# A down projection by 26 products on blocks of 188 columns instead of 20 on 251, and where its sums and copies are issued

## Chip, cores and metric

The kernel runs on one core of a Trainium2 chip. The metric is the device time of one execution in microseconds, the median of several runs. The engines are TensorE (PE, with its weight loads shown apart as PEld), VectorE (DVE), ScalarE (ACT), GpSimd (POOL) and SyncE (SP), which issues the DMAs. TensorE reads its operands from SBUF and writes to PSUM banks; VectorE and ScalarE read and write both.

## What is computed

The reference, cut to what matters (all float32):

```python
# x: (8, 3008, 256), w_in: (256, 2048), w_out: (2048, 256)
X = np.fft.fft(x, axis=1)
X = np.fft.fft(X, axis=2)
x = X.real.reshape(8 * 3008, 256)
h = x @ w_in
g = np.maximum(0.01 * h, h)
return g @ w_out
```

So a two-dimensional Fourier transform of each of eight sequences, its real part, an up projection to 2048 features, a leaky ReLU and a down projection to 256.

## The kernel before, in words

**Up.** The transform along the features is folded into the weights once, at the start, so `wf` holds a cosine half and a sine half of the up projection. The real part of the transform at frequency k and at its mirror S - k are the sum and the difference of the same two products. Per unit (one of the 8 sequences and one parity of k, 16 units in all) the transform along the sequence leaves two tiles, `mixc` and `mixs`. The head of the kernel handles 502 columns of the first unit plainly (lines 864 to 917). All else is done in 31 *chunks* of up to 377 columns, two per unit except in the first. `Chunk.up` (line 1050) makes, for each of 16 blocks f of 128 hidden features, a cosine product and a sine product of 377 columns (line 1053); `seed` (line 1048) has put the Nyquist term into the cosine bank beforehand. ScalarE copies the cosine bank to SBUF (line 1061), and `hidden` (line 1064) has VectorE write copy + sine and copy - sine to the tile `block` (line 1075). One step later ScalarE applies the leaky ReLU in place (line 1324).

**Down.** A chunk gives 2 x 377 or 2 x 376 outputs. They are cut into 3 blocks of 251 columns; the 16 hidden blocks are taken as 4 groups of 4 (`divmod(f, 4)`: group k, row g), and the 256 outputs as 2 halves. The down projection is thus a product of a 2x4 by a 4x3 matrix of blocks, 24 block products, each of four rows g. It is done with 20, in the manner of Strassen: `W_SUMS` lists sums of weights (made once, line 651), `SUMS` the sums of hidden blocks, `PRODUCTS` triples of (weight, value, accumulator), and `COMBINED` the sums and differences of accumulators, of which `RESULTS` are the outputs.

- `sum` (line 1090) makes one sum of hidden blocks on GpSimd (line 1095), 4 x 251 = 1004 elements on 128 partitions. A sum is written over an operand that is used for the last time, or into a free slot. In the last chunk every third sum goes to VectorE.
- `product` (line 1101) makes one row of one product on TensorE (line 1112), 251 columns, into one half of one of three PSUM banks, `sum_psa`, `sum_psb`, `sum_psc`. The trace shows a float32 product as two records.
- `combine` (line 1121) is called when both accumulators of a bank are complete: ScalarE copies those in `COPIED` to SBUF (line 1128), and what can be combined goes on a list. `make` (line 1148) makes one combination on VectorE (line 1156), from PSUM or from SBUF. `leave` (line 1140) makes what is left in a bank before the bank is written again. `put` (line 1178) stores a result by DMA from SP.
- `Slots` (line 979) hands out 24 places in `block`: three adjacent ones for a group k, one for a sum.

**Transform along the sequence.** Beside this, x of the next sequence is loaded and folded (lines 378 to 406), and turned and multiplied for the next unit (`transform`, line 1189). VectorE's part goes through the queue `folds` (class `Later`, line 919). `by_turns` (line 934) sends every third fold to VectorE with both inputs in SBUF (line 932), and for the two others ScalarE first copies one input to PSUM (line 940) and VectorE takes it from there (line 930). The `None` behind a copy in the queue (line 941) ends a call of `emit`, so that the copy's reader is issued only at the next call.

**Order.** All engines run their instructions in the order in which this Python code issues them. `rest` (line 1244) sorts events by a time in *steps*: a step is one f of one chunk, 16 to a chunk. Within a chunk that begins at 0, the up product of f is at 1.2 + f, the sums at `SUMS_AT` (from 14.43 on, so they overlap the next chunk's up products), and row m of the products at 18 + m/5. At each full step `go_on` advances the transform, and `some(1)` issues combinations and folds with both inputs in SBUF up to a budget in us; after each up product `some(0)` does so for those that read PSUM. A GpSimd sum waits for the last VectorE operation with both inputs in SBUF that was issued ahead of it (`gate`, line 971), whether it needs its data or not.

Of the kernel before, what the change touches and what calls it, by code (L numbers as in the profile page):

```python
# [57 lines left out]
    (6, 1, -1), (2, 1, -1), (0, 3, -1), (6, 7, 1), (4, 5, 1), (2, 6, -1), (5, 1, -1), (0, 1, 1), (2, 3, 1),  # L58
    (0, 4, -1), (1, 4, 1), (3, 6, 1), (3, 4, -1), (3, 7, -1), (4, 7, -1), (6, 5, -1),
]  # L60
SUMS = [
    (4, 7, 1, 14.43), (8, 12, 1, 15.4), (8, 7, 1, 16.37), (0, 3, -1, 17.34), (15, 13, -1, 18.31),
    (3, 5, -1, 19.29), (6, 8, -1, 20.26), (9, 18, -1, 21.23), (12, 19, 1, 22.2), (1, 10, 1, 23.17),
    (0, 17, -1, 24.14), (19, 21, 1, 25.11), (22, 2, -1, 26.09), (11, 21, 1, 27.06), (24, 25, -1, 28.03),
    (11, 10, 1, 30.43),
]
PRODUCTS = [
    (8, 13, 0), (9, 14, 1), (10, 1, 1), (1, 16, 2), (11, 9, 3), (12, 17, 3), (13, 8, 4), (14, 5, 5), (6, 20, 6),
    (15, 0, 7), (16, 18, 7), (17, 2, 8), (18, 22, 9), (3, 23, 10), (19, 19, 11), (4, 26, 12), (20, 25, 13), (21, 11, 14),
    (22, 27, 15), (23, 4, 15),  # L70
]
COMBINED = [
    (6, 11, -1), (10, 16, 1), (0, 2, -1), (5, 18, 1), (13, 17, -1), (9, 19, 1), (4, 18, 1), (14, 20, -1), (22, 7, 1),
    (24, 16, -1), (1, 0, -1), (26, 4, -1), (27, 17, 1), (22, 8, 1), (29, 9, 1), (30, 12, -1), (31, 20, 1), (3, 6, -1),
    (33, 21, 1), (23, 15, -1), (21, 12, -1), (36, 23, -1),
]
RESULTS = [25, 28, 32, 34, 35, 37]
COPIED = [0, 3, 6]
NA = 16

SUMS_AT = [x[3] for x in SUMS]
UP_FROM, DOWN_FROM, PER_STEP = 1.2, 18, 5
ON_POOL, ON_VECTOR, AHEAD, X_AHEAD, TRANSFORM_FROM, TURNS = 0.8, 1.2, 1, 2, 10, 3
TRIPLES, PARTS = 8, 14
SELF = 2 * KB[0]
# [151 lines left out]
def chunks():  # L237

    plain, at = [], 0
    for j in range(PLAIN):  # L240
        plain.append((0, PARITIES[0], j * CW, CW, at))
        at += 2 * CW
    chunk = []
    for u, (b, c) in enumerate((b, c) for b in range(B) for c in PARITIES):
        for lo, hi in ((PLAIN * CW, UW[c]),) if u == 0 else ((0, KW[c]), (KW[c], UW[c])):
            n = -(-2 * (hi - lo) // 3) if hi - lo < KW[0] else CW
            chunk.append((u, lo, hi - lo, n, at))
            at += 3 * n
    return plain, chunk, at


def columns():
# [4 lines left out]
    pieces = [(b, c, j, n, first) for b, c, j, n, first in plain]  # L257
    for u, j, m, _, first in chunk:
        pieces.append((*units[u], j, m, first))
    for b, c, j, m, first in pieces:  # L260
        col = j + np.arange(m)
        once = np.arange(m) - (np.arange(m) > SELF if m == KW[0] else 0)
# [3 lines left out]
        at[b * S + minus] = first + m + once  # L266
# [5 lines left out]
def tile_fnet_leaky_relu(  # L272
# [22 lines left out]
    block_sb = const.tile([P, TRIPLES * 4 * 3 * CW], F32, name="block")  # L295
    part_sb = const.tile([P, PARTS * CW], F32, name="part")
# [129 lines left out]
    class Rows:  # L426
# [23 lines left out]
        def fold_odd(self, v=nc.vector, sc=None):  # L450
            x, y, z = self.src[:, 4:6], self.src[:, 6:8], self.z
            if self.c == 1:
                for i in range(2):
                    turn(x[:, i], y[:, i], 1 + i, self.part, (z(2 + 2 * i), z(3 + 2 * i)), (z(8 + 2 * i), z(9 + 2 * i)), v, sc)
                v.tensor_tensor(z(12, 2), z(8, 2), z(10, 2), op=ALU.add)
# [463 lines left out]
    class Later:  # L919
# [14 lines left out]
        def by_turns(self, to, x, y, op):  # L934
# [6 lines left out]
            self.queue.append(None)  # L941
# [9 lines left out]
        def emit(self, us):  # L951

            while self.queue:
                if self.queue[0] is None:
                    self.queue.pop(0)
                    return
                cost, pool, call = self.queue[0]
                if pool is not None:
                    if us[pool] < cost / 2:
                        return  # L960
                    us[pool] -= cost
                self.queue.pop(0)
                call()

# [14 lines left out]
    class Slots:  # L979


        def __init__(self):
            self.free = set(range(3 * TRIPLES))

        def left(self, i):
            return sum(j in self.free for j in range(i // 3 * 3, i // 3 * 3 + 3))

        def take(self):
            i = min(self.free, key=lambda i: (self.left(i), i))
            self.free.remove(i)  # L990
            return i

        def take_three(self):
            i = min(i for i in self.free if self.left(i) == 3)
            self.free -= {i, i + 1, i + 2}
            return i
# [4 lines left out]
        def rows(self, i):  # L1001
            return block_sb[:, i // 3 * 12 * CW : (i // 3 + 1) * 12 * CW].rearrange("p (g n) -> p g n", g=4)

        def place(self, i, n):
            return self.rows(i)[:, :, i % 3 * CW : i % 3 * CW + n]

    class Parts:
# [10 lines left out]
        def __getitem__(self, i):  # L1018
            return part_sb[:, i * CW : (i + 1) * CW]
# [3 lines left out]
    def uses_of_values():  # L1023
        n = [0] * (12 + len(SUMS))
# [7 lines left out]
    class Chunk:  # L1032
# [3 lines left out]
        def __init__(self, t):  # L1036
            self.u, self.j, self.m, self.n, self.first = chunk[t]
            self.twice = self.m == KW[0]
            self.w = self.m if self.twice else 3 * self.n - self.m
# [10 lines left out]
        def up(self, f):  # L1050
# [5 lines left out]
            if g == 0:  # L1056
                first = block.take_three()
                for j in range(3):
                    self.at[3 * k + j] = first + j
# [4 lines left out]
        def hidden(self, k, g, copy, sin):  # L1064
            row = block.rows(self.at[3 * k])[:, g]
            parts = [(0, 0, self.m, ALU.add)]
            if self.twice:
                parts += [(self.m, 0, SELF, ALU.subtract), (self.m + SELF, SELF + 1, self.m, ALU.subtract)]
            else:
                parts += [(self.m, 0, self.w, ALU.subtract)]  # L1070
            for to, lo, hi, op in parts:
                while lo < hi:
                    at = to // self.n * CW + to % self.n
                    end = hi if self.n == CW else min(hi, lo + self.n - to % self.n)
                    nc.vector.tensor_tensor(row[:, at : at + end - lo], copy[:, lo:end], sin[:, lo:end], op=op)  # L1075
                    to, lo = to + end - lo, end
            if self.n == CW:
                return row
            return row.rearrange("p (j n) -> p j n", j=3)[:, :, 0 : self.n]
# [10 lines left out]
        def sum(self, i, engine=None):  # L1090
# [3 lines left out]
            self.at[12 + i] = free.pop(0) if free else block.take()  # L1094
            ins = (engine or nc.gpsimd).tensor_tensor(self.value(12 + i), xa, ya, op=ALU.add if sign > 0 else ALU.subtract)  # L1095
# [25 lines left out]
        def combine(self, bank):  # L1121

            n, here = self.n, (2 * bank, 2 * bank + 1)
# [54 lines left out]
        def put(self, v):  # L1178
            d, j = divmod(RESULTS.index(v), 3)
# [64 lines left out]
    def rest():  # L1244
# [4 lines left out]
        for t in range(count):  # L1249
            for f in range(NF):  # L1250
                events.append((16 * t + UP_FROM + f, 3, t, f))
            for i, s in enumerate(SUMS_AT):
                events.append((16 * t + s, 1, t, i))
# [43 lines left out]
        for _, kind, t, i in events:  # L1297
            if kind == 0:
# [4 lines left out]
                if t == count and waiting:  # L1303
                    to = waiting.pop()
                    nc.scalar.activation(to, to, ACT.Lrelu)
                go_on(16 * t + i)
                some(1)
                if t >= count:
                    some(0)
            elif kind == 1:  # L1310
                every[t].sum(i, nc.vector if t == count - 1 and i % 3 == 2 else None)
# [5 lines left out]
            else:  # L1317
# [5 lines left out]
                for to in waiting:  # L1323
# [233 lines left out]
```

## Time and profile before

| | us |
|---|---|
| median of 3 runs | 1857.11 (1857.03 to 1857.15) |
| the profiled execution | 1857.0 |
| its span in the trace | 1855.2 |
| TensorE busy | 1840.8 |
| VectorE busy | 1122.9 |
| ScalarE busy | 1081.7 |
| GpSimd busy | 1069.1 |
| first up product of a chunk starts at | 124.8 |
| last one starts at | 1813.0 |

The span is what the trace covers; the profiled execution's own time is 1.8 us more. The granted TensorE clock was 0.999. Lines in the views name an engine, a line of the code, the tile written and the tiles read (`sum_psa<-block,wt`), the shape and the number of instructions. Durations are those of single records; consecutive records of one engine can overlap, so a rate is read from the starts in the timeline, not from the mean duration. DMA moved 88 MB, on average 48 GB/s.

### The profile page before, as it was taken

To read this page: it belongs to the slowest core of one execution; us is meant where nothing else is said; L and a number is where in the kernel's file an instruction comes from. 1 tells how busy PE (TensorE), PEld (TensorE's weight loads), DVE (VectorE), ACT (ScalarE), POOL (GpSimd) and SP (SyncE) were. 2 spreads that over 40 slices of the span, in tenths; PEclk is the share of its full clock that TensorE was granted. 3 is DMA by queue.
4 is the path that set the end of the run, shared out by engine and by line. 5 is a ranking of instruction groups with operands and counts; after the bars stand their busy time and mean duration, and the time that the engine had idled before them with its cause. 6 is when DMAs were issued, how large, how long until landed. Compare 5 with 4: busy or idle time off the path is not lost.

```text
span 1855.2 us, 22815 instructions
## 1 busy us (share of the span) xinstructions
PE 1840.8 (99%) x7936; PEld 1454.7 (78%) x7936; DVE 1122.9 (61%) x2688; ACT 1081.7 (58%) x1951; POOL 1069.1 (58%) x533
## 2 busy tenths in 40 slices
PE   9999999999999999999999999999999999999999
PEld 7786777777777777877777777777777777777777
DVE  8957766575555755557555665646656566455444
ACT  3448665565655656566565665656665575555550
POOL 1224665656665656565656656656656556656664
PEclk9999999999999999999999999999999999999999
DMA  6312121100212001120100212002120100010000
GB/s 233 116 34 98 29 71 34 65 15 25 71 34 71 16 25 65 34 71 30 61 22 27 71 34 71 16 21 69 34 71 28 49 31 31 26 34 18 9 12 31
DMA packets 56946, 88.32 MB, mean 48 GB/s; under 512 B 8048, under 2 KB 44528, under 8 KB 56832
## 3 DMA queue, kind: packets, MB, share of 16 engines
q1 hardware_dynamic: 56688, 86.88, 14.2%
q8 instruction: 62, 1.02, 0.2%
q14 instruction: 52, 0.43, 0.1%
q10 hardware_dynamic: 144, 0.00, 0.0%
HBM read 62.12 MB, written 24.72 MB: 47 GB/s over the span
## 4 chain that ended last, share of the span: by engine, by line
PE 93%; DVE 3%; ACT 1%; DMA 1%; issue 1%; POOL 0%; DVEq 0%; SPq 0%; ACTq 0%; POOLq 0%
PE sum_psb L1112 18%; PE sum_psa L1112 18%; PE sum_psc L1112 18%; PE cos_psa L1053 8%; PE cos_psb L1053 8%; PE sin_psb L1053 8%; PE sin_psa L1053 8%; PE dft_ps L689 3%; PE sum_psc L911 1%; PE sum_psa L911 0%; PE dft_ps L911 0%; PE sum_psb L911 0%; DVE block L1075 0%; DMA block<-in_w_out_dram 0%; ACT cos L1061 0%
## 5 line engine op out<-in xcount | busy, mean ns | idle before, releaser
L1095 POOL TENSOR_TENSOR block<-block 128x1004 f32<-128x1004 f32 (+1 forms) x491 | 1040.6, 2131 | 689.5 <-DVE part L1156 209.3
L1075 DVE TENSOR_TENSOR block<-cos,sin_psb 128x376 f32<-128x376 f32 (+5 forms) x576 | 251.7, 484 | 383.5 <-PE sin_psb L1053 375.8
L1075 DVE TENSOR_TENSOR block<-cos,sin_psa 128x376 f32<-128x376 f32 (+5 forms) x576 | 251.9, 485 | 271.1 <-PE sin_psa L1053 221.7
L1324 ACT ACTIVATE block<-block 128x753 f32<-128x753 f32 (+1 forms) x494 | 399.7, 809 | 0.1
L1112 PE MATMUL sum_psb<-block,wt 128*128 128x251 f32 (+1 forms) x1336 | 314.4, 372 | 0.0
L1112 PE MATMUL sum_psa<-block,wt 128*128 128x251 f32 (+1 forms) x1328 | 313.5, 372 | 0.0
L1112 PE MATMUL sum_psc<-block,wt 128*128 128x251 f32 (+1 forms) x1304 | 309.7, 373 | 0.0
L1112 PEld LDWEIGHTS sum_psb<-block,wt 128*128 128x128 f32 x1336 | 249.5, 189 | 53.9
L1112 PEld LDWEIGHTS sum_psa<-block,wt 128*128 128x128 f32 x1328 | 248.2, 189 | 54.0
L1112 PEld LDWEIGHTS sum_psc<-block,wt 128*128 128x128 f32 x1304 | 244.5, 189 | 53.4
L1061 ACT COPY cos<-cos_psa 128x377 f32<-128x377 f32 (+1 forms) x248 | 116.4, 469 | 238.1 <-PE cos_psa L1053 235.7
L1061 ACT COPY cos<-cos_psb 128x377 f32<-128x377 f32 (+1 forms) x248 | 116.1, 468 | 222.8 <-PE cos_psb L1053 221.7
L1053 PE MATMUL cos_psa<-mixc,wf 128*128 128x377 f32 (+1 forms) x496 | 196.4, 478 | 2.0 <-ACT cos_psa L1048 2.0
L1053 PE MATMUL cos_psb<-mixc,wf 128*128 128x377 f32 (+1 forms) x496 | 196.4, 477 | 1.4 <-ACT cos_psb L1048 1.4
L1053 PE MATMUL sin_psa<-mixs,wf 128*128 128x377 f32 (+1 forms) x496 | 196.1, 477 | 0.0
L1053 PE MATMUL sin_psb<-mixs,wf 128*128 128x377 f32 (+1 forms) x496 | 196.0, 477 | 0.0
L1048 ACT ACTIVATE cos_psa<-nb,wn 128x377 f32<-128x377 f32 (+1 forms) x248 | 142.8, 576 | 8.1
L1048 ACT ACTIVATE cos_psb<-nb,wn 128x377 f32<-128x377 f32 (+1 forms) x248 | 142.7, 576 | 8.1
L1053 PEld LDWEIGHTS sin_psa<-mixs,wf 128*128 128x128 f32 x496 | 93.8, 190 | 61.9 <-DVE block L1075 1.0
L1053 PEld LDWEIGHTS sin_psb<-mixs,wf 128*128 128x128 f32 x496 | 93.7, 190 | 61.9 <-DVE block L1075 0.7
L940 ACT COPY dft_ps<-xt 128x512 f32<-128x512 f32 (+1 forms) x112 | 65.8, 588 | 71.5 <-DVE xt L930 71.5
L1053 PEld LDWEIGHTS cos_psa<-mixc,wf 128*128 128x128 f32 x496 | 93.0, 189 | 14.8 <-ACT cos_psa L1048 4.2
(219 smaller groups left out, 1747.7 us busy)
## 6 DMA issues: line engine op xcount, KB each, us to landing
xt<-in_x_dram SPq DMA_DIRECT2D x28, 1024.0 KB, 6.8
out_dram<-part SPq DMA_DIRECT2D x180, 125.5 KB, 1.8
tabe<-in_seq_tab_dram SPq DMA_DIRECT2D x29, 190.0 KB, 2.7
nb<-nyq_dram SPq DMA_DIRECT2D x23, 188.0 KB, 3.7
block<-in_w_in_dram SPq DMA_DIRECT2D x8, 512.0 KB, 6.0
block<-in_w_out_dram SPq DMA_DIRECT2D x8, 512.0 KB, 6.1
xt<-in_first_x_dram SPq DMA_DIRECT2D x4, 768.0 KB, 8.0
tabo<-in_seq_tab_dram SPq DMA_DIRECT2D x15, 191.0 KB, 2.7
```

Of the source, the lines that this page charges most:

```text
L689: nc.tensor.matmul(o, lhsT=still, rhs=moving, start=(i == 0), stop=(i == 3), skip_group_check=True)
L911: nc.tensor.matmul(sums[j][d][:, r * n : (r + 1) * n], lhsT=wo[:, fs[h] // 4, fs[h] % 4, d], rhs=a[r][h], start=(f == 0 and r == 0 and h = ...
L940: self.queue.append((0.0, None, lambda: nc.scalar.copy(copy, y)))
L1048: nc.scalar.activation(cos_ps[f % 2][:, 0 : self.w], columns_of(nb_sb, self.u, self.j, self.w), ACT.Copy, scale=wn[:, f : f + 1])
L1053: nc.tensor.matmul(bank[:, 0 : self.w], lhsT=wf[:, i, f * P : (f + 1) * P], rhs=columns_of(mix_sb[i], self.u, self.j, self.w), start=(i == ...
L1061: nc.scalar.copy(copy, cos[:, 0 : self.w])
L1075: nc.vector.tensor_tensor(row[:, at : at + end - lo], copy[:, lo:end], sin[:, lo:end], op=op)
L1095: ins = (engine or nc.gpsimd).tensor_tensor(self.value(12 + i), xa, ya, op=ALU.add if sign > 0 else ALU.subtract)
L1112: nc.tensor.matmul(to, lhsT=weight(w)[:, g], rhs=self.value(v)[:, g], start=(first and at == 0), stop=(last and g == 3), skip_group_check= ...
L1324: nc.scalar.activation(to, to, ACT.Lrelu)
```

## The change

The outputs of a chunk are cut into 4 blocks instead of 3, of 188 columns (189 for a chunk of 377, 125 for the first chunk), and the 16 hidden blocks of rows are seen as 4 groups of 4 as before. The down projection becomes a product of a 2x4 by a 4x4 matrix of blocks, 32 block products, done with 26. New tables give 18 sums of weights instead of 16, 28 sums of hidden blocks instead of 16, 26 products instead of 20, 24 accumulators instead of 16, 34 combinations instead of 22, 8 results instead of 6, and 8 accumulators copied by ScalarE instead of 3.

Ten of the 28 sums of a chunk go to VectorE, at their own places in the order; they do not enter the gate of GpSimd's sums. The places of the sums are given apart from the table. Products are spread at 6.5 rows a step from 18.1 on.

Each value has a slot of its own in `block`, 28 in all; the four values of a group take four free slots, evenly spaced where there are such, else any. `hidden` writes a row by two instructions, one for copy + sine and one for copy - sine, each into two slots, and the leaky ReLU of a row is one instruction for four evenly spaced slots, else two.

In the queue of folds, ScalarE's copies are issued by `emit_copies` alone, right after an up product and its seed and ahead of the leaky ReLU; `emit` stops at a copy. `together` puts the scaled copies of the odd rows ahead of their readers. Every second fold by turns, instead of every third, has both inputs in SBUF; budgets go to 1.2 us for both sorts, and the transform of a unit may begin at step 8 of a chunk instead of 10.

```diff
@@ -55,34 +55,37 @@
...
-RESULTS = [25, 28, 32, 34, 35, 37]
-COPIED = [0, 3, 6]
-NA = 16
-
-SUMS_AT = [x[3] for x in SUMS]
-UP_FROM, DOWN_FROM, PER_STEP = 1.2, 18, 5
-ON_POOL, ON_VECTOR, AHEAD, X_AHEAD, TRANSFORM_FROM, TURNS = 0.8, 1.2, 1, 2, 10, 3
-TRIPLES, PARTS = 8, 14
-SELF = 2 * KB[0]
+RESULTS = [39, 41, 44, 46, 48, 51, 53, 57]
+COPIED = [0, 1, 2, 3, 4, 6, 14, 20]
+NA = 24
+
+SUMS_AT = [14.51, 15.26, 16.05, 16.0, 16.74, 17.24, 17.74, 18.73, 18.48, 19.22, 19.47, 20.71, 20.32, 21.56, 22.06, 22.67, 22.04, 24.14, 24.64, 25.38, 25.37, 27.17, 27.22, 28.21, 29.08, 30.06, 30.17, 31.54]
+UP_FROM, DOWN_FROM, PER_STEP, LATER = 1.20, 18.10, 6.5, 0
+BY_VECTOR = (0, 3, 6, 8, 9, 12, 16, 17, 21, 25, )
+ON_POOL, ON_VECTOR, AHEAD, X_AHEAD, TRANSFORM_FROM, TURNS = 1.20, 1.20, 1, 2, 8, 2
+SLOTS, RS, SS, PARTS = 28, 191, 764, 24
...
-            n = -(-2 * (hi - lo) // 3) if hi - lo < KW[0] else CW
+            n = (hi - lo + 1) // 2
             chunk.append((u, lo, hi - lo, n, at))
-            at += 3 * n
+            at += 4 * n
...
             if self.c == 1:
+                since = len(folds.queue)
                 for i in range(2):
                     turn(x[:, i], y[:, i], 1 + i, self.part, (z(2 + 2 * i), z(3 + 2 * i)), (z(8 + 2 * i), z(9 + 2 * i)), v, sc)
+                folds.together(since)
...
             self.queue.append((0.0, None, lambda: nc.scalar.copy(copy, y)))
-            self.queue.append(None)
             self.tensor_tensor(to, x, copy, op)
...
             while self.queue:
-                if self.queue[0] is None:
-                    self.queue.pop(0)
+                cost, pool, call = self.queue[0]
+                if pool is None or us[pool] < cost / 2:
                     return
-                cost, pool, call = self.queue[0]
-                if pool is not None:
-                    if us[pool] < cost / 2:
-                        return
-                    us[pool] -= cost
+                us[pool] -= cost
                 self.queue.pop(0)
                 call()
+
+        def emit_copies(self):
+
+            while self.queue and self.queue[0][1] is None:
+                self.queue.pop(0)[2]()
+
+        def together(self, since):
+
+            late = self.queue[since:]
+            self.queue[since:] = [x for x in late if x[1] is None] + [x for x in late if x[1] is not None]
...
+        def take_four(self):
+            fours = self.fours()
+            r = sorted(fours[0]) if fours else sorted(self.free)[0:4]
+            self.free -= set(r)
+            return r
...
+        def rows(self, r, g, n):
+            steps = {y - x for x, y in zip(r, r[1:])}
+            return [self.row(a, g, n) for a in ([r] if len(steps) == 1 else [r[0:2], r[2:4]])]
...
+            r = [self.at[4 * k + j] for j in range(4)]
+            x, y = (a.rearrange("p (j n) -> p j n", j=2) for a in (copy, sin[:, 0 : self.w]))
+            for to, op in ((r[0:2], ALU.add), (r[2:4], ALU.subtract)):
+                nc.vector.tensor_tensor(block.row(to, g, self.n), x, y, op=op)
+            return block.rows(r, g, self.n)
...
             elif kind == 1:
-                every[t].sum(i, nc.vector if t == count - 1 and i % 3 == 2 else None)
+                every[t].sum(i, nc.vector if i in BY_VECTOR or t == count - 1 and i % 3 == 2 else None)
...
                 seed(16 * t + i + 2)
-                for to in waiting:
+                folds.emit_copies()
+                for to in sum(waiting, []):
                     nc.scalar.activation(to, to, ACT.Lrelu)
```

## Prediction

> **What bounds the kernel now.** I read the page's busy shares and its chain first.
>
> ```profile
> PE 1840.8 (99%) x7936; PEld 1454.7 (78%) x7936; DVE 1122.9 (61%) x2688; ACT 1081.7 (58%) x1951; POOL 1069.1 (58%) x533
> PE sum_psb L1112 18%; PE sum_psa L1112 18%; PE sum_psc L1112 18%; PE cos_psa L1053 8%; PE cos_psb L1053 8%; PE sin_psb L1053 8%; PE sin_psa L1053 8%; PE dft_ps L689 3%; PE sum_psc L911 1%; PE sum_psa L911 0%; PE dft_ps L911 0%; PE sum_psb L911 0%; DVE block L1075 0%; DMA block<-in_w_out_dram 0%; ACT cos L1061 0%
> ```
>
> TensorE is busy for 99% of the span, and its own instructions make up nearly the whole chain that ended last; the three sum banks, which are the down projection that the change rewrites, hold 54% of it. Next, who makes TensorE wait (engine and line, waited for whom: us in total, times, longest):
>
> ```profile
> PE cos_psa L1053 <- ACT cos_psa L1048: 2.0, 4, 1.4
> ...
> PE sum_psa L1112 <- POOL block L1095: 0.7, 1, 0.7
> ```
>
> Over the whole run the products waited 0.7 us for a sum. By the table of stretches TensorE was busy 1684.90 of the 1689 us from the first up product (124) to the last (1813): that stage is TensorE's stream. Then what one matrix product takes. The groups split by shape give the latency of one record:
>
> ```profile
> L1112 PE MATMUL sum_psa<-block,wt 128*128 128x251 f32 x1280 | 305.4, 375 | 0.0
> L1112 PE MATMUL sum_psb<-block,wt 128*128 128x167 f32 x56 | 9.2, 304 | 0.0
> ```
>
> That mean is not the price, because products overlap. The price is the distance between starts, in the timeline (start, us, what, count), here of two stretches:
>
> ```profile
> 999.74 0.94 PE L689 MATMUL dft_ps<-tabe,xt 95*128 95x95 f32 x7
> 1000.52 0.62 PE L1112 MATMUL sum_psc<-block,wt 128*128 128x251 f32 x2
> ...
> 1002.24 2.28 PE L1112 MATMUL sum_psc<-block,wt 128*128 128x251 f32 x10
> 1004.36 0.80 PE L1053 MATMUL cos_psb<-mixc,wf 128*128 128x377 f32 x2
> ```
> ```profile
> 195.94 1.01 PE L1112 MATMUL sum_psb<-block,wt 128*128 128x167 f32 x6
> 196.80 0.41 PE L1112 MATMUL sum_psc<-block,wt 128*128 128x251 f32 x1
> ```
>
> Ten products of 251 columns take 1004.36 - 1002.24 = 2.12 us, 212 ns each; six of 167 take 0.86 us, 143 ns; seven of 95 take 0.78 us, 111 ns. From 251 to 167 it falls by 69/84 = 0.82 ns a column, so about 2.8 ns of each is not streaming (212 - 251/1.2). Below that line lies a floor: 95 columns would be 82 ns and are 111.
>
> **The products (removed and added).** Each product call leaves 2 records for each of 4 rows of blocks: 20 x 8 = 160 records per chunk before (the 4,800 of the 30 full chunks agree), 26 x 8 = 208 after. A chunk of 376 columns gives blocks of 188, one of 377 gives 189. On the line above these cost 159.5 and 160.3 ns. Before: 160 x 0.212 = 33.95 us per chunk. After: 208 x 0.1595 = 33.17 (22 chunks), or 208 x 0.1603 = 33.34 (8 chunks). The up products, 64 records per chunk, go from 377 columns to 376 or 378: -0.05 or +0.05 us. Gain: 22 x (0.78 + 0.05) + 8 x (0.61 - 0.05) = 22.7 us. The first chunk goes from 160 records at 142 (22.7) to 208 of 125 columns; streaming says 107 ns, the floor 111, so 23.1 us: a loss of 0.4. Net 22.3 us, all of it on the path.
>
> A rule could speak against 48 more weight loads per chunk. The Trainium skill (TensorE: Matmul & The Clock Gate, LDWEIGHTS) prices a load at columns/1.2, so 107 ns for 128. If it stood beside the stream, 188 columns would cost 264 ns and 251 would cost 316: 54.9 against 50.6 us, 4.3 us a chunk lost. The row of 143 ns at 167 columns says the load is hidden there (in sum it would be 246), and the 111 ns at 95 columns is where it shows. I take the row.
>
> **The 18 sums on GpSimd and 10 on VectorE.** The rows of line 1095, and of the combinations that have both inputs in SBUF (xcount: min/median/max ns):
>
> ```profile
> L1095 POOL TENSOR_TENSOR block<-block x491: 1365/1977/3282, 146.7 to 1844.1; 128x1004 f32<-128x1004 f32 x158, 128x668 f32<-128x668 f32 x6
> L1095 DVE TENSOR_TENSOR block<-block x5: 1192/1200/3296, 1814.5 to 1838.9; 128x1004 f32<-128x1004 f32 x5
> ```
> ```profile
> L1156 DVE TENSOR_TENSOR part<-part x186: 320/414/2539, 180.9 to 1851.7; 128x251 f32<-128x251 f32 x180, 128x167 f32<-128x167 f32 x6
> ```
>
> GpSimd's mean by shape is 2152 ns at 1004 elements and 1493 at 668, so 1658 at 752: 18 x 1.66 = 29.8 us a chunk, against 16 x 2.15 = 34.4 now. It gets lighter. VectorE's sum took 1200 ns at 1004 when nothing held it; 752 is 0.90 by proportion, 0.94 with some fixed part. So +9.4 us a chunk. The maximum of 3296 is the price of a collision: 2.1 us, one GpSimd sum.
>
> **The combinations.** 22 of 251 become 34 of 188, of which 15 instead of 6 have both inputs in SBUF. Before: 16 x 0.41 + 6 x 0.52 = 9.7 us. A VectorE operation from PSUM on 188 columns took 0.345 (346 and 342 ns at line 930): 34 x 0.345 = 11.7. +2.0 us. Hidden rows of the 377 chunks go from three operations (1.07 us in the timeline) to two (1.00 at 376): -1.1 us in every fourth chunk.
>
> **VectorE's sum.** The stretches of one cycle (length, PE, PEld, DVE, ACT, POOL busy):
>
> ```profile
> 1244.00:1300.00 56.00, 56.00 (x235) 44.04 (x234) 35.85 (x86) 37.34 (x65) 34.24 (x16) 1.00 0.17 59
> ...
> 1412.00:1468.00 56.00, 56.00 (x250) 44.43 (x249) 31.24 (x79) 30.69 (x58) 34.14 (x16) 1.00 0.10 28
> ```
>
> VectorE is busy 31.2 to 35.9 us of 56, on average 1006/30.2 = 33.3. With 9.4 + 2.0 - 0.3 it comes to 44.4 on average and 47 in the heaviest, of a TensorE period that becomes 55.2. That covers the sums if waiting stays small, and this is the disputed cost, the SBUF port. In the trace a combination from SBUF has mean 520 and median 414: 0.11 us of waiting. The Trainium skill (SBUF — State Buffer, section "SBUF: two separate sides") states an exclusive lock: a VectorE operation with two SBUF inputs and a GpSimd operation block each other for the whole instruction. By the rule, an operation that arrives at random finds GpSimd busy 29.8/55.2 = 0.54 of the time and waits half of 1.66 us: 0.45 us. I count 35 such operations a chunk (10 sums, 15 combinations, about 10 folds). Rule: 35 x 0.45 = 15.7 us, so 60 on average, over the period. Row: 35 x 0.11 = 3.9. The arrivals are not random: line 971 makes a GpSimd sum wait for the last VectorE operation from SBUF ahead of it, so GpSimd runs beside the hidden rows, whose copy is in SBUF and whose other input is in PSUM (542 ns median with GpSimd busy 61%, maximum 552: no collision). Most VectorE sums stand right behind such an operation or behind the hidden row. The new sums have no gate of their own, so I take 0.15 us, nearer the row: some 48 us a chunk, 87% of the period. Ends: 0.11 and 0.45.
>
> What queues behind a late VectorE: the hidden row (line 1075), so the sine bank that TensorE wants again two steps later (6.9 us; about 5 may be lost), and the sums, due 1.4 to 2.2 steps after their place (at least 4.8 us, of which 0.9 is the sum). A lateness under about 4 us costs TensorE nothing. In a step with folds VectorE holds 1.0 + 0.94 + 1.4 + 0.7 = 4.1 us where it has a sum (10 of 16 steps) and 3.1 where not, of 3.45: lateness rises and falls by 1 to 3 us. I charge 2 us of stalls in all for it (ends 0 and 40).
>
> **ScalarE and the copies.** Per b, folds by turns keep 12 of 16 copies (588 ns each), the other four become folds from SBUF (732 against 679 ns on VectorE). Eight part copies for three cost +1.5 us a chunk; leaky ReLUs of three of four groups split in two where the four slots are not evenly spaced (12 x 0.25 = +3 us). ScalarE's 30.7 to 37.3 goes to at most 42 of 55: hidden. A copy one step behind its predecessor's reader stops waiting for VectorE (71.5 us of ScalarE idle now), which moves nothing on TensorE; its cover is the 13 us of idle, and without it the next cosine seed would be late. On SP the outputs go from 6 to 8 per chunk, each behind the combination it waits for; loads of tables and x, with 2.7 and 6.8 us to landing, follow them two steps ahead of use. Nothing. Two more sums of weights (line 651, 1.35 us each) fall into GpSimd's 72.6 us of waiting for line 591: nothing; without that cover 2.7 us, once.
>
> **Slots.** 28 slots hold 16 hidden values a chunk where 24 held 12. Following the order of taking and freeing, the fifth hidden row of a chunk is written to a slot that GpSimd's sum 27 read half a step earlier, so VectorE may wait there for GpSimd, and with it the rest of its queue. Its nearest row is line 1075's wait for line 1095, 7.1 us in 5 times (1.4 us each). Ends 0 and 30 x 1.4 = 42 us on VectorE, within the 4 us of allowed lateness each time: 0 on TensorE. The transform begins at step 8 instead of 10 and folds come at two a step: its SP loads move two steps up, ahead of outputs that are not awaited.
>
> **Ends.** After the last product the last bank feeds 6 dependent combinations instead of 3: 6 x 0.34 - 3 x 0.41 = +0.8 us. In the tail (1813 to 1855) a step takes 2.1 us, so due times shrink to 2.9 us: +1. In the first chunk VectorE is at 41 of 56 already: +1 for stalls.
>
> Sum on the profiled execution: span 1855.2 - 22.3 + 0.8 + 1 + 1 + 2 = 1837.7, and with the 1.8 around it (1857.0 - 1855.2) 1839.5; the median of the runs lies 0.1 above the profiled run. Before's own 4.1 us of TensorE idle between 124 and 1813 could shrink a little with the late copies. I say 1839.
>
> **Rivals.**
> - VectorE's bursts bite, but seldom: where x is folded (21 bursts of eight folds), each costs TensorE about 0.5 us: 10 us given back, 1849. For it: 4.1 us in a step of 3.45. Against: record means overstate, as VectorE operations overlap by some 0.08 us.
> - Slower: the port makes VectorE the bound, in the chunk loop. VectorE's period passes the present 56 us once the waits exceed (56 - 44.4)/35 = 0.33 us an operation; at the rule's 0.45 it is 60, so +4 x 30 = 1977. It decides from 0.33 on; the maximum of 3296 speaks for it, the median 414 against.
> - The products do not get cheaper: if one cost its record's mean (322 ns at 188), 208 x 0.322 - 160 x 0.375 = +7 us a chunk, 2067. The starts exclude it.
> - No change: stalls of 0.7 us a chunk eat the 22 us; 1857.
>
> **How the numbers follow.** 1839 has 0.66, bursts 0.14, no change 0.05, slower 0.15. The range runs from the pure stream (1857.1 - 22.3 is 1835, less some of the old idle: 1832) to the bursts at double size, 1853. A measurement of this kernel can tell about 0.2% from no change.
>
> **What would show it.** Right: starts of sum products 159 to 161 ns apart; TensorE at 99% with chunks of 55.2 us; VectorE's busy time near 48 per chunk; sums on VectorE near 0.94 us with a few above 2. Wrong: TensorE waiting at line 1053 for line 1075, or at line 1112 for VectorE's sums, by more than 10 us in total, or product starts over 165 ns apart without a wait.

## The result, and the profile after

In its first timing the changed kernel took 1840.78, 1841.19 and 1844.83 us, and the ratio to the kernel before is 0.992, 95% interval 0.99 to 0.9939. A fourth execution of that timing, the profiled one, ran TensorE's products more than two times longer throughout (3897.31 us) and is left out here, though with it the median of the four is 1843.01. A second timing gave a median of 1843.26 (1841.49 to 1845.34) and 0.9928 (0.9915 to 0.994); the profile after is from it: 1845.23 us, span 1843.4. The change is faster by 0.7 to 0.8%; the forecast was 1839, with 1832 to 1853 as its range.

Its page, first the busy shares and the chain by engine:

```profile
span 1843.4 us, 27101 instructions
...
PE 1824.6 (99%) x9424; PEld 1546.9 (84%) x9424; DVE 1554.9 (84%) x3212; ACT 1123.4 (61%) x2298; POOL 1103.2 (60%) x595
...
PE 92%; DVE 5%; issue 1%; ACT 1%; DMA 1%; POOL 1%; POOLq 0%; SPq 0%; DVEq 0%; ACTq 0%
```

TensorE is at 99% again, now with 9424 records of products instead of 7936. VectorE went from 61% to 84%, ScalarE from 58% to 61%, GpSimd from 58% to 60%. In the chain that ended last, VectorE's share is 5% now. What TensorE waited for (total, times, longest):

```profile
PE sum_psc L1115 <- POOL block L1098: 3.4, 1, 3.4
...
PE sin_psb L1068 <- DVE block L1081: 1.0, 1, 1.0
```

A single wait of 3.4 us is new, near the end of the run; the sine bank, which a late VectorE would hold up, cost 1.0 us. The starts of products in the timeline, of a full chunk and of the first chunk:

```profile
1003.31 0.79 PE L1068 MATMUL cos_psb<-mixc,wf 128*128 128x376 f32 x2
1003.94 0.80 PE L1068 MATMUL sin_psb<-mixs,wf 128*128 128x376 f32 x2
1004.58 1.12 PE L1115 MATMUL sum_psc<-block,wt 128*128 128x188 f32 x6
1005.53 1.44 PE L1115 MATMUL sum_psa<-block,wt 128*128 128x188 f32 x8
1006.81 0.79 PE L1068 MATMUL cos_psa<-mixc,wf 128*128 128x376 f32 x2
```
```profile
185.99 1.50 PE L1115 MATMUL sum_psc<-block,wt 128*128 128x125 f32 x12
187.33 0.80 PE L1068 MATMUL cos_psb<-mixc,wf 128*128 128x378 f32 x2
```

Six products of 188 columns take 1005.53 - 1004.58 = 0.95 us and the next eight 1.28: 158 and 160 ns each, where 251 columns took 212. The median distance from one start to the next is 159 ns at 188 columns and 160 at 189, over the whole trace. Twelve of 125 columns take 1.34 us, 112 ns each.

By stretches (length, then busy us of PE, PEld, DVE, ACT, POOL, then the granted clock):

```profile
124.00:240.00 116.00, 111.63 (x611) 89.42 (x610) 101.81 (x231) 87.93 (x189) 55.54 (x33) 1.00 0.19 65
240.00:1783.00 1543.00, 1543.00 (x8039) 1315.79 (x8038) 1309.29 (x2721) 976.84 (x2020) 986.37 (x504) 1.00 0.13 41
1783.00:1843.00 60.00, 51.72 (x287) 48.53 (x285) 42.24 (x80) 9.72 (x21) 29.52 (x14) 0.94 0.08 25
```

From 240 to 1783 the records of TensorE leave no gap; a record lasts longer than the distance between starts, so a wait of a tenth of a microsecond would not show. From 124 to 240 TensorE is idle for 4.4 us, and in the last stretch the granted clock falls to 0.94. Where the 11.8 us between the two spans come from, by the starts of chunks in the two traces:

| | before | after | difference |
|---|---|---|---|
| start to the first up product | 124.8 | 126.4 | +1.6 |
| first chunk's and second chunk's up products | 69.6 | 71.7 | +2.1 |
| 28 chunks | 1566.9 | 1544.7 | -22.2 |
| last chunk's up products | 51.7 | 50.9 | -0.8 |
| last up product to the end | 42.2 | 49.7 | +7.5 |

A full chunk went from 55.96 to 55.17 us. The two ends gave back nearly half of what the middle gained.

### The profile page after: what moved, and what is told of

Same layout as the page of the kernel before. It is cut to its first block, busy times and chain, and to the rows that moved or that the text cites. A ratio compares the mean times of both kernels' runs of the same rounds, so it can differ in the third digit from the quotient of the medians.

```text
span 3895.5 us, 27101 instructions
## 1 busy us (share of the span) xinstructions
PE 3889.6 (100%) x9424; PEld 2809.1 (72%) x9424; DVE 1459.8 (37%) x3212; ACT 1132.7 (29%) x2298; POOL 1053.7 (27%) x595
## 4 chain that ended last, share of the span: by engine, by line
PE 100%; DVE 0%; issue 0%; POOL 0%; DVEq 0%; POOLq 0%
PE sum_psc L1115 22%; PE sum_psa L1115 17%; PE sum_psb L1115 17%; PE sin_psb L1068 9%; PE cos_psa L1068 9%; PE sin_psa L1068 9%; PE cos_psb L1068 9%; PE dft_ps L693 2%; PE sum_psa L915 1%; PE sum_psc L915 1%; PE sum_psb L915 1%; PE dft_ps L915 1%; PE sum_psa L1359 0%; PE cos_psb L880 0%; PE cos_psa L880 0%; PE sin_psb L880 0%
## 5 line engine op out<-in xcount | busy, mean ns | idle before, releaser
L1098 POOL TENSOR_TENSOR block<-block 128x752 f32<-128x752 f32 (+2 forms) x551 | 1025.3, 1871 | 2641.9 <-DVE xt L936 559.5
L1115 PE MATMUL sum_psc<-block,wt 128*128 128x188 f32 (+2 forms) x1736 | 660.1, 552 | 0.0
L1115 PE MATMUL sum_psa<-block,wt 128*128 128x188 f32 (+2 forms) x1736 | 640.4, 552 | 0.0
L1329 ACT ACTIVATE block<-block 128x376 f32<-128x376 f32 (+4 forms) x714 | 421.7, 620 | 0.0
L1068 PE MATMUL cos_psa<-mixc,wf 128*128 128x376 f32 (+2 forms) x496 | 391.6, 906 | 0.0
L1068 PE MATMUL sin_psb<-mixs,wf 128*128 128x376 f32 (+2 forms) x496 | 391.0, 903 | 0.0
L1068 PE MATMUL cos_psb<-mixc,wf 128*128 128x376 f32 (+2 forms) x496 | 388.8, 879 | 0.0
L1068 PE MATMUL sin_psa<-mixs,wf 128*128 128x376 f32 (+2 forms) x496 | 387.4, 879 | 0.0
L1115 PE MATMUL sum_psb<-block,wo 128*128 128x188 f32 (+2 forms) x992 | 378.0, 552 | 0.0
L1115 PE MATMUL sum_psb<-block,wt 128*128 128x188 f32 (+2 forms) x992 | 364.8, 553 | 0.0
```

Source lines behind the costliest of these rows:

```text
L1068: nc.tensor.matmul(bank[:, 0 : self.w], lhsT=wf[:, i, f * P : (f + 1) * P], rhs=columns_of(mix_sb[i], self.u, self.j, self.w), start=(i == ...
L1098: ins = (engine or nc.gpsimd).tensor_tensor(self.value(16 + i), xa, ya, op=ALU.add if sign > 0 else ALU.subtract)
L1115: nc.tensor.matmul(to, lhsT=weight(w)[:, g], rhs=self.value(v)[:, g], start=(first and at == 0), stop=(last and g == 3), skip_group_check= ...
```

## The experiments

Ratios are to the kernel before on the same chip; the waits and stretches are those of each kernel's profiled execution.

**The changed kernel unaltered.**

> The changed kernel unaltered, for a profile at the usual speed of TensorE. My theory (the time is TensorE's stream, and narrower blocks shorten it): 1841 us, starts of sum products 159 to 161 ns apart, under 12 us of TensorE waiting in all, VectorE busy some 48 us of a 55 us chunk. The rival theory (the port between VectorE and GpSimd decides): waits of 0.3 us and more on each VectorE operation with two SBUF inputs, and TensorE waiting at line 1068 for line 1081.

Measured: 1843.26 us, 0.9928 (0.9915 to 0.994), as shown above. Product starts and VectorE's load (1309.29 us of the 1543 in the middle, so 46.8 us a chunk) are what the theory of TensorE's stream expected; the waits listed for TensorE add up to 13.8 us, a little over the 12. How often VectorE and GpSimd met at the port is seen in the sums and in the combinations with both inputs in SBUF:

```profile
L1098 DVE TENSOR_TENSOR block<-block 128x752 f32<-128x752 f32 x227 | 293.3, 1294 | 5.4 <-POOL block L1098 5.4
L1159 DVE TENSOR_TENSOR part<-part 128x188 f32<-128x188 f32 x330 | 134.8, 445 | 2.2 <-ACT part L1131 1.0
```

A VectorE sum took 1.29 us on average. Where no GpSimd sum was running at its start it took 0.93, so a sum waited some 0.36 us; a combination from SBUF took 0.445, and 0.347 in the median, so it waited 0.10.

**All sums on GpSimd.**

```diff
-BY_VECTOR = (0, 3, 6, 8, 9, 12, 16, 17, 21, 25, )
+BY_VECTOR = ()
```

> All 28 sums on GpSimd, but for the last chunk's third on VectorE as before. My theory: GpSimd then holds 28 x 1.66 = 46 us of a 55 us chunk before it waits for anything, and its waits for the last VectorE operation from SBUF bring it over the period: TensorE waits for sums at line 1115, some 3 us a chunk, 1930 us (range 1870 to 2000). The rival (VectorE's extra load and the port cost the missing 6 us): VectorE falls back to 35 to 40 us a chunk and the time to 1836.

Measured: 1944.62 us, 1.0474 (1.0459 to 1.0488).

```profile
PE 1853.0 (95%) x9424; PEld 1553.0 (80%) x9424; DVE 1510.3 (78%) x2904; ACT 1125.6 (58%) x2298; POOL 1581.6 (81%) x903
```
```profile
PE sum_psc L1115 <- POOL block L1098: 67.3, 47, 3.3
```
```profile
L1159 DVE TENSOR_TENSOR part<-part 128x188 f32<-128x188 f32 x330 | 316.4, 995 | 2.7 <-ACT part L1131 1.4
```

GpSimd is busy for 1581.6 us and TensorE waits for its sums. VectorE got only 45 us lighter in all, since most of what it saves on sums it loses waiting: its combinations from SBUF took 995 ns now instead of 445. So the table with 26 products needs VectorE's share of the sums. The rival falls.

**The copies as before.** In the changed kernel, a copy again ends a call of `emit`, and the readers are issued at the next; `emit_copies` does nothing, and `together` is not called (both left out below).

```diff
             self.queue.append((0.0, None, lambda: nc.scalar.copy(copy, y)))
+            self.queue.append(None)
...
-                cost, pool, call = self.queue[0]
-                if pool is None or us[pool] < cost / 2:
-                    return
+                if self.queue[0] is None:
+                    self.queue.pop(0)
+                    return
```

> The changed kernel with ScalarE's copies for folds issued as before (a call of emit ends behind a copy, no separate place, no reordering of the odd rows' copies). My theory: the copies move ScalarE's idle time and little else, TensorE is within a few us: 1843 us (1840 to 1850). The rival (the copies carry part of the gain, because a hidden row waits behind a fold that waits for its copy): 1853 us or more, with VectorE waiting for line 944 in each fold.

Measured: 1848.38 us (1847.72 to 1849.37), 0.9954 (0.994 to 0.9968): 5.1 us slower than the changed kernel, timed beside it. That lies inside my range and short of the rival's 1853, but well clear of the 1843 that I expected. ScalarE's wait for the reader of the copy before is back:

```profile
ACT dft_ps L943 <- DVE xt L933: 63.0, 70, 2.0
```
```profile
ACT dft_ps L944 <- DVE xt L934: 2.1, 3, 1.1
```

It is 63.0 us here (first line) and 2.1 us in the changed kernel (second line). Most of what TensorE loses by it lies at the start of the chunk stage. The stretch from 110 to 240 us, of this kernel and of the changed one:

```profile
110.00:240.00 130.00, 120.93 (x646) 96.60 (x645) 112.08 (x238) 90.25 (x192) 60.37 (x47) 1.00 0.17 58
```
```profile
110.00:240.00 130.00, 125.13 (x673) 101.12 (x672) 113.36 (x245) 92.00 (x197) 66.76 (x50) 1.00 0.17 58
```

TensorE is idle for 9.1 us against 4.9, which is 4.2 us of difference in two executions whose medians are 5.1 apart.

**The late copies alone, on the kernel before** (with the settings of the folds that the change has).

```diff
-ON_POOL, ON_VECTOR, AHEAD, X_AHEAD, TRANSFORM_FROM, TURNS = 0.8, 1.2, 1, 2, 10, 3
+ON_POOL, ON_VECTOR, AHEAD, X_AHEAD, TRANSFORM_FROM, TURNS = 1.2, 1.2, 1, 2, 8, 2
...
-            self.queue.append(None)
...
                 seed(16 * t + i + 2)
+                folds.emit_copies()
```

The new `emit`, `emit_copies` and `together` go with it and are left out here.

> The kernel before with the change's queue of copies alone (and its settings for the folds: turns of 2, budgets of 1.2 us, transform from step 8); products and sums as before. My theory: TensorE had 4.1 us of idle between the first and the last up product, so 1857 us, at best 1855. The rival (late copies gain by themselves): 1850 us or less.

Measured: 1853.6 us (11 runs, 1853.28 to 1853.99), 0.9982 (0.9973 to 0.9991). My theory allowed 1855 at best, so it falls for this part; the rival's 1850 was not reached either. Before, and with the late copies:

```profile
110.00:240.00 130.00, 125.91 (x593) 98.58 (x592) 91.10 (x260) 93.28 (x188) 62.53 (x44) 1.00 0.17 58
```
```profile
110.00:240.00 130.00, 128.06 (x610) 101.19 (x609) 91.46 (x264) 92.28 (x186) 63.40 (x45) 1.00 0.17 58
```

TensorE's idle time in this stretch went from 4.1 to 1.9 us.

**The settings alone, on the kernel before:** the first pair of lines of that diff.

> The kernel before with the change's settings for the folds alone (turns of 2, budget 1.2 us for operations from SBUF, transform from step 8), copies issued as before. The late copies with these settings took 3.5 us off. If the gain is the copies' place: 1857 us. If it is the settings': 1854 us.

Measured: 1857.92 us (1856.13 to 1858.63), 1.0004 (0.9995 to 1.0013). So the settings alone gain nothing, and the 3.5 us come with the place of the copies. Late copies with the old settings were not run.

**No gate for GpSimd's sums.**

```diff
-            if engine is None:
-                wait_for_gate(ins)
```

> No gate for any GpSimd sum, so that GpSimd starts as soon as its data are there. By the theory that the gate is what keeps the waits at the port small, VectorE's operations from SBUF wait 0.3 us and more each instead of 0.1 to 0.36, VectorE's busy time passes 50 us a chunk and TensorE waits: 1860 us (1848 to 1900). By the rival (the port is rarely met in any order) the time stays within 2 us of 1843.

Measured: 1941.29 us (1940.57 to 1941.63), 1.0452 (1.0436 to 1.0468).

```profile
L1157 DVE TENSOR_TENSOR part<-part 128x188 f32<-128x188 f32 x330 | 253.1, 803 | 1.8 <-ACT part L1129 0.6
```
```profile
PE sin_psa L1068 <- DVE block L1081: 36.9, 14, 4.9
PE sin_psb L1068 <- DVE block L1081: 15.9, 19, 2.7
```
```profile
L1081 DVE TENSOR_TENSOR block<-cos,sin_psa 128x376 f32<-128x376 f32 x352 | 175.1, 537 | 79.4 <-PE sin_psa L1068 79.3
```
```profile
1000.00 3.65 POOL L1098 TENSOR_TENSOR block<-block 128x752 f32<-128x752 f32 x2 [2.42 <-PE sum_psb L1113]
```
```profile
1001.01 2.85 DVE L1157 TENSOR_TENSOR part<-part 128x188 f32<-128x188 f32 x2
```
```profile
240.00:1860.00 1620.00, 1554.55 (x7965) 1309.29 (x7964) 1478.30 (x2705) 967.45 (x2007) 966.49 (x500) 0.99 0.12 39
```

That is slower than my whole range, 1848 to 1900. A combination of 188 columns from SBUF took 803 ns instead of 445: it waits 0.46 us instead of 0.10. A hidden row, which reads one operand from PSUM, took 537 ns, as with the gate (540). The two timeline lines show one wait: two GpSimd sums run from 1000.00 to 1003.65, and the second of the two combinations that began at 1001.01 ends at 1003.86, 0.21 us behind the second sum. VectorE is busy for 1478 of 1620 us and TensorE waits for the hidden rows, 52.8 us for these two banks; a chunk takes 58.6 us. This is the slower rival of the prediction, brought about by one edit. The 52.8 us are not the whole loss of 98: TensorE waits some 24 us more for other work of VectorE, and the rest is not listed as waits.

**The kernel before without its gate:** the same two lines.

> The kernel before without the gate of GpSimd's sums. There VectorE has 33 us of work in a chunk of 56 and meets the port with some 16 operations a chunk instead of 35. By the theory that the missing gate costs an operation from SBUF about 0.45 us, VectorE gets 16 x 0.35 = 6 us heavier, to 39 of 56, and TensorE hardly notices: 1858 us (1856 to 1864). The rival (the gate guards something else, such as sums that come too late by waiting behind one another): 1880 us or more.

Measured: 1872.14 us (1871.53 to 1872.39), 1.008 (1.0064 to 1.0096), between the two expectations. The combinations from SBUF before, and without the gate:

```profile
L1156 DVE TENSOR_TENSOR part<-part 128x251 f32<-128x251 f32 x180 | 91.2, 520 | 15.1 <-ACT part L1128 15.1
```
```profile
L1154 DVE TENSOR_TENSOR part<-part 128x251 f32<-128x251 f32 x180 | 203.8, 1145 | 8.9 <-ACT part L1126 8.9
```
```profile
PE sin_psb L1053 <- DVE block L1075: 7.1, 9, 2.7
PE sin_psa L1053 <- DVE block L1075: 2.1, 7, 0.7
```

Here a combination from SBUF went from 520 to 1145 ns, by 0.62 us, more than the 0.35 that I had put in. I had taken the 0.45 us of the changed kernel; this kernel's sums are longer (2.15 us) and hold GpSimd for 34.4 of 56 us, so the same rule gives 0.61 x 2.15 / 2 = 0.66 us, and 0.55 more than the row of 0.11. VectorE's busy time rose by 1418.6 - 1122.9 = 296 us, 10 us a chunk, and TensorE waited 9.2 us for hidden rows. The same mechanism, with the size missed. The gate mattered before as well, by 15 us, and in the changed kernel it matters by 98.

**VectorE's sums in the gate as well.**

```diff
             if engine is None:
                 wait_for_gate(ins)
+            else:
+                gate.append(ins)
```

> VectorE's sums enter the gate as well: a GpSimd sum waits also for a sum on VectorE issued ahead of it. If the 0.36 us that a VectorE sum waits comes from GpSimd sums that start just before it, it falls to about 0.1 us and VectorE gets 2 to 3 us a chunk lighter, with no gain on TensorE in the middle, where it does not wait: 1843 us (1840 to 1847). The rival (GpSimd becomes late by the added waits): 1850 us or more.

Measured: 1866.2 us (1865.66 to 1867.26), 1.0049 (1.0036 to 1.0063). The rival was right.

```profile
POOL block L1098 <- DVE block L1098: 487.9, 253, 6.2
```
```profile
L1098 DVE TENSOR_TENSOR block<-block 128x752 f32<-128x752 f32 x227 | 287.0, 1266 | 7.2 <-POOL block L1098 7.0
L1161 DVE TENSOR_TENSOR part<-part 128x188 f32<-128x188 f32 x330 | 180.0, 582 | 2.2 <-ACT part L1133 1.0
```
```profile
PE sum_psc L1117 <- POOL block L1098: 20.5, 15, 4.1
```

GpSimd waits 487.9 us for VectorE's sums instead of 111.0, TensorE 20.5 us for GpSimd's. And the sum on VectorE is hardly shorter, 1266 for 1294 ns, while the combinations went from 445 to 582. So a GpSimd sum held back does not vanish: it meets other operations of VectorE instead. By the starts and ends of records, 102 of the 227 VectorE sums of 752 elements began while a GpSimd sum was running (122 in the changed kernel), but 88 of the 330 combinations of 188 columns (60 there), and each of those waited longer.

**No gate in the last chunk.** GpSimd's sums of the last chunk wait for their data alone.

```diff
-            if engine is None:
+            if engine is None and self is not every[-1]:
```

> The changed kernel with GpSimd's sums of the last chunk not waiting for the last VectorE operation from SBUF (their data they wait for as before). My theory: the 3.4 us of TensorE waiting for a GpSimd sum in the tail, and the stretch of half clock behind it (6.8 us at 0.5), come from that gate, so some 5 us go: 1838 us, and the granted clock of all runs at 0.998 or more. The rival (the sums are late because sums of both engines shut each other out of SBUF): no gain or a loss, 1843 to 1846 us.

What it is aimed at are these lines of the changed kernel's tail, of TensorE and of GpSimd, and the stretches around them:

```profile
1801.72 1.44 PE L1115 MATMUL sum_psb<-block,wo 128*128 128x188 f32 x8
1806.56 2.88 PE L1115 MATMUL sum_psc<-block,wo 128*128 128x188 f32 x8 [3.40 <-POOL block L1098]
1809.23 4.15 PE L1115 MATMUL sum_psc<-block,wt 128*128 128x188 f32 x16
```
```profile
1802.49 9.92 POOL L1098 TENSOR_TENSOR block<-block 128x752 f32<-128x752 f32 x4 [5.05 <-DVE part L1159]
```
```profile
1797.00:1803.00 6.00, 6.00 (x39) 5.87 (x37) 5.86 (x14) 0.89 (x3) 0.95 (x2) 1.00 0.21 67
1803.00:1812.00 9.00, 5.60 (x18) 5.44 (x18) 5.61 (x5) 0.53 (x2) 9.00 (x4) 0.63 0.07 22
```

GpSimd stood idle for 5.05 us until a combination on VectorE (line 1159) was done, then ran four sums back to back; TensorE waited 3.40 us for one of them. When it went on, eight products of 188 columns took 2.67 us, 334 ns each instead of 160: the granted clock is 0.63 over these 9 us, since it stood at half for 6.8 us.

Measured without the gate there: 1839.16 us (1837.41 to 1840.07), 0.9902 (0.9888 to 0.9915), with a clock of 0.998 to 1.0, as expected. TensorE's waits in the tail are 1.4 and 1.0 us, for VectorE's sums. It is the fastest version of the study, ahead of both kernels; against the changed kernel its gain of 4 us is about what the two intervals, which meet at 0.9915, can tell apart. The stretch from the last up product to the end says it more clearly. It took 45.2 to 45.3 us in the three profiles without this gate (this one, the last one below, and the one without any gate), and 48.7 to 51.0 us in the five versions of the changed kernel that had it.

**The last chunk split as all others.**

```diff
-nc.vector if i in BY_VECTOR or t == count - 1 and i % 3 == 2 else None
+nc.vector if i in BY_VECTOR else None
```

> The last chunk splits its sums between the engines as all others do (10 on VectorE, 18 on GpSimd), without the further third on VectorE. If VectorE's lateness in the tail makes the gate late, this helps: 1840 us. If GpSimd's 18 x 1.6 us in 37 us of tail are too many, it costs: 1846 to 1850 us.

Measured: 1844.38 us (1843.87 to 1845.22), 0.9931 (0.9919 to 0.9944). No gain, and neither of the two expectations: TensorE's waits for GpSimd in the tail are then 5.8 us in six pieces of at most 2.2. GpSimd has more sums there and still its gate, so this does not tell the two causes apart.

**No gate in the last chunk, and the first chunk's sums all on GpSimd.**

```diff
-nc.vector if i in BY_VECTOR or t == count - 1 and i % 3 == 2 else None
+nc.vector if t > 0 and i in BY_VECTOR or t == count - 1 and i % 3 == 2 else None
```

> As the version without the gate in the last chunk, and in the first chunk all 28 sums on GpSimd. If VectorE's load is what makes TensorE wait 4.9 us between 110 and 240 us, about 2 us go: 1837 us. If GpSimd, with 28 x 1.25 = 35 us, becomes late there, it costs: 1841 us or more.

Measured: 1840.45 us (1837.69 to 1841.1), 0.9909 (0.9895 to 0.9923), not to be told from the version before it. TensorE is busy for 125.11 of the 130 us from 110 to 240, and 125.14 in that version. So taking VectorE's sums away gains nothing there, and the expectation was a miss.

## Why the prediction was right, point by point

**The products: right, and exact.** Forecast 159.5 and 160.3 ns, measured medians 159 and 160; the first chunk 111, measured 112. The forecast drew its line at 1/1.2 = 0.83 ns a column, where its own two rows gave 0.82; from 188 to 251 columns the medians give 0.83. The sum for 28 full chunks gave about 21 us (0.76 each), and 22.2 came. The mean of a record at 188 columns is 322 ns in the profile after, just what the third rival assumed as the price; it is latency, and the rival was rightly excluded by the starts. The weight load beside 188 columns stays hidden, as the row of 167 had said.

**VectorE's load: right.** Forecast 48 us a chunk with 0.15 us of waiting per operation from SBUF; it was 46.8. Over all 1076 operations from SBUF (sums, combinations and folds, 35 a chunk) the wait was 0.17 us. But the forecast thought the new sums sheltered, as they stand behind other VectorE work, and looked for sums near 0.94 us with a few above 2. Half of them took over 1 us, and a sum waited 0.37 on average over all shapes, nearer the rule's 0.45 than the row's 0.11; combinations (0.11) and folds (0.06) made up for it. So the average is right partly by luck.

**Row or rule, and why.** The records show the lock that the prediction quotes. A VectorE operation with both inputs in SBUF that begins while a GpSimd sum is running ends at a nearly fixed time behind that sum (four in five of them within 0.03 us): 0.21 us at 188 columns, 0.28 at 251, 0.80 for a sum of 752 elements. One that begins at any other time takes its usual 0.345, 0.41 or 0.93 us. Hidden rows take 0.54 us in both cases. Counted from the starts and ends of records:

| | operations from SBUF | begun during a GpSimd sum | mean wait of those, us | mean over all, us |
|---|---|---|---|---|
| before | 457 | 57 | 0.82 | 0.10 |
| before, no gate | 457 | 279 | 1.12 | 0.68 |
| changed | 1076 | 312 | 0.59 | 0.17 |
| changed, no gate | 1076 | 374 | 1.03 | 0.36 |
| changed, all sums on GpSimd, with gate | 768 | 426 | 0.86 | 0.48 |

So the forecast did well to stay near the row, because the gate makes arrivals anything but random, as the prediction said. The last line shows the limit: with GpSimd busy for 81% of the span, the same gate left 0.48 us. The rule's size at random is less sure. It fits before (0.66 against 0.68); in the changed kernel it gave 0.45, and without the gate the mean is 0.36, with 0.42 on combinations, 0.33 on sums and 0.30 on folds. That the combinations of 188 columns alone came to 0.46 is chance.

Of the slower rival the decisive point was 0.33 us, and its time at 0.45 was 1977; the kernel without a gate, at 0.36, took 1941. Its mechanism came about only in part: VectorE's load rose to 53.5 us a chunk (1478 of 1620), not to 60, and stayed under the chunk's 58.6. By the waits listed, TensorE lost its time mostly to hidden rows that came late now and then (33 waits, up to 4.9 us), before VectorE was full.

**Lateness in the middle: mis-sized, to the good.** 2 us charged for it, and rival one put 10 on the bursts of folds. The records show no wait of TensorE from 240 to 1783.

**The tail: mis-sized.** The prediction put +0.8 for the last combinations and +1 for tighter due times; it was +7.5. The step "due times shrink to 2.9 us: +1" left the gate out of the tail, where a GpSimd sum waits for a VectorE combination of the chunk before that it has no use for. With the gate taken out of the last chunk +3.0 is left. Of the other 4.5 us, 4.2 are accounted for: in the profile after, TensorE waits 3.8 us for GpSimd in the tail and loses about 2.8 of the 5.6 us that it then runs at half clock; without the gate it waits 2.4 us for VectorE.

**The copies: put at nothing, and wrongly.** "Moves nothing on TensorE" was said of them; they are worth 5.1 us in the changed kernel and 3.5 in the one before. The cover that I named, ScalarE's 13 us of idle time per chunk, is an average over the middle. At the start of the chunk stage VectorE is busy for 112 of 130 us. There a copy that waits for its predecessor's reader (6.2 us in 10 times from 110 to 240 with the copies as before) can hold up the seed behind it: TensorE waits 4.5 us for seeds in that stretch, and 2.0 with the late copies. In the kernel before, the gain is part of the 4.1 us of idle that "could shrink a little". In the changed one it is more than that: with the old copies the first two chunks take 75.3 us, against 71.7, and 69.6 before the change.

**How much of the number was luck.** The forecast gave all of its 18 us to the products and nothing to the copies. Products, sums and combinations with the copies as before give 8.7 us (1848.38); the copies bring the other 5.1. So the tail's unforeseen 5.7 us and a gain that was put at nothing nearly cancel. Even 1848.38 lies in the range, whose upper end was drawn for bursts of folds, which did not come.

**The first chunk: +1.4 said, +2.1 measured**, for the first two chunks together. What TensorE still waits for there, 4.9 us from 110 to 240, is open: taking VectorE's sums away did not change it. The head's +1.6 is not the change's: among the eight profiles with the changed kernel's head, the first up product starts at 123.0 us where the clock was never at half in the head, at 124.6 to 125.1 where it was for 3.4 us, and at 125.4 to 126.4 where it was for 6.8. The profile after has 6.8 us, the one before 3.4.

## What to carry to other kernels

Price a product by the distance between starts at two widths, never by its record; 48 more records of products per chunk cost nothing beyond their columns at 188, while at 125 columns the distance no longer shrinks with them (112 ns, as 111 at 95). When one engine's work is moved to another, ask what orders the two at a shared port: here a wait that no data require was worth 98 us over the whole run, and the same wait cost some 4 us in the tail, where TensorE soon needs the sum that it holds back. Cover named for a moved copy has to be looked up in the stage where the engine is fullest, not in the average.

## What the hardware showed unexpectedly

Apart from one at the very end of a run, the stretches at half clock in these traces last 3.4 or 6.8 us each, and the same wait does not always bring the same stretch. In the tail, a wait of 3.40 us came with 6.8 us at half clock in the profile after (334 ns instead of 160 for 188 columns), and with 3.4 us in the kernel with the copies as before. In the head, one wait of 2.8 us on the weights (line 629 for line 595) came with no such stretch in one of the eight profiles, with 3.4 us in four and with 6.8 in three.

The Trainium skill (TensorE: Matmul & The Clock Gate, "Why this matters for your kernels") warns of idle gaps over about 3 us. From the first chunk on, all ten waits of 3.3 us or more came with half clock, which agrees; but shorter ones did too, so 3 us is no safe limit here. With all sums on GpSimd, twelve such waits were between 2.42 and 2.94 us, and the clock dropped at six of them. One with a drop, of 2.46 us, and one without, of 2.90 us (TensorE's line, then the stretch around it with its granted clock, third number from the end):

```profile
748.85 2.67 PE L1115 MATMUL sum_psc<-block,wo 128*128 128x188 f32 x8 [2.46 <-POOL block L1098]
```
```profile
746.00:753.00 7.00, 4.54 (x17) 4.13 (x16) 3.17 (x6) 2.60 (x6) 6.31 (x5) 0.76 0.00 0
```
```profile
866.58 1.54 PE L1115 MATMUL sum_psc<-block,wo 128*128 128x188 f32 x8 [2.90 <-POOL block L1098]
```
```profile
864.00:871.00 7.00, 4.42 (x24) 3.91 (x25) 3.94 (x8) 3.81 (x10) 7.00 (x5) 1.00 0.01 2
```

The mean clock also orders the runs of the unaltered kernel: 0.996 in those of 1844.8, 1845.2 and 1845.3 us, 0.997 at 1843.3, 0.998 at 1841.5 and 1842.7, 0.999 at 1840.8 and 1841.2. Its spread goes with the time at half clock, then. Whether that time lay in the head or in the tail is known only for the profiled executions, and what decides its length is open.
